# Start addresses of the weight buffers in SBUF: 0 modulo 512 bytes, or odd multiples of 16

## The chip, the core and the metric

The kernel runs on one core of a Trainium2 chip. The metric is device time in microseconds, from the start to the end of one launch. TensorE (PE) multiplies, VectorE (DVE), ScalarE (ACT) and GpSimd (POOL) do the work between the products, SyncE (SP) issues nearly all DMAs. SBUF is the on-chip memory that all engines read; PE writes its sums to PSUM.

## The reference

Attention with 4 sink tokens and a window of 128 over 4 x 8 heads, then a mixture of 8 experts over the 3072 tokens that it gives, every expert on every token, weighted by a Sinkhorn-normalised gate:

```python
x = attn_out.transpose(0, 2, 1, 3).reshape(3072, 512)
P = exp(x @ w_gate - max);  8 times: rows to sum 1, columns to sum N / E
for e in range(8):
    h = np.maximum(x @ w1[e], 0.0)        # 512 -> 1024
    out += P[:, e:e+1] * (h @ w2[e])      # 1024 -> 512
```

All of it is float32.

## The kernel before, in words

The tokens are worked in three parts of 1024; the code numbers them 0, 1, 2, and the change speaks of the second and third of these (`part` 1 and 2 in the code). Each expert's 1024 hidden columns are cut into four units of 256, so a part has 32 units. Both products of a unit are done by a Strassen-Winograd scheme with seven smaller products, M1 to M7. Each number is held as a float32 pair, high and low (`fp32r` tiles with an index of 2 in them), and a product is the sum of three terms: high by high, high by low, low by high.

In the first part the sums of weight blocks that the scheme needs (the weights' forms) are made on the chip and stored in DRAM (`w1s`, `w2s`). In the other two parts they are only loaded again, one form at a time, 128 partitions by 2 KB. The first product's form goes to a buffer of pool `w1q` (8 buffers, tile name W1q, issued in `load_w1`), the second product's form to a buffer of pool `w2q` (16 buffers, tile name W2q, issued in `load_w2`). A buffer that has been used is loaded again at once for a later product.

Each matmul has its own 128x128 block of weights: it is loaded into the array by an LDWEIGHTS (PEld in the profile) while the matmul before it runs, and then 512 columns of the other operand stream past it. In these parts the weights are always slices of W1q or W2q. What streams is a form of x for the first product (tiles B11, B21, B22, T1 to T4; line L902, in `product`), and a form of the hidden values for the second (tiles hf, pool `hq`; line L1467, in `second2`). One Strassen product is six such matmuls, and the blocks of one buffer lie 512 bytes apart:

```python
TERMS = [(0, k, b) for k in range(KH) for b in range(2)] + [(1, k, 0) for k in range(KH)]
    for j, (a, k, b) in enumerate(TERMS):
        nc.tensor.matmul(ps, lhsT=w1(a, k), rhs=x[:, b, k, :], ...)
```

The six of the second product take three from each of two units' buffers. The order of the work is written out by hand (`ORDER`, `SECOND`, `STEPS2`, and `at`, which puts an action some steps later), so nothing in it depends on addresses. Two unused tiles, `pad` and `base`, bring the pools on the left and on the right side of SBUF to multiples of 512 bytes: in the built program every tile that PE reads in the three parts (W1f, W2f, h, W1q, W2q, hf and the forms of x) starts at 0 modulo 512.

The attention ahead of the parts has tiles that don't. The scores (L498, in `scores`) take keys as the streaming operand and queries as the weights from one tile KQ, which holds for each of two (high, low) and two pairs of heads a row of 516 floats: 260 of keys, then 256 of queries. Two heads go side by side on 64 partitions each, so matmuls come in pairs. The transposes of the probabilities (L530, in `transpose_p`) take as weights `sc[:, h, SINK:]` for eight heads, whose rows are 132 floats (528 bytes) long; what streams there is always the same identity matrix.

Of the kernel before, what the change touches and what calls it, by code (L numbers as in the profile page):

```python
# [10 lines left out]
F32R = mybir.dt.float32r  # L11
# [5 lines left out]
P = 128  # L17
# [221 lines left out]
def tile_sink_attention_moe(ctx: ExitStack, tc: tile.TileContext, q, k, v, wg, w1, w2, out):  # L239
# [15 lines left out]
    KH = KC // 2  # L255
# [7 lines left out]
    def f32(ap):  # L263
        return ap.bitcast(F32)
# [118 lines left out]
    for hh in range(2):  # L383
        t = att2.tile([P, NP, CW + 2 * P], F32, name=f"KQF{hh}")
# [520 lines left out]
    HD = DM // 2  # L905
    weighted = []
    W1Q = {}
# [34 lines left out]
    w1p, cp, rawp, sp, xrp = (pool_(*a) for a in (("w1p", 1), ("cp", 1), ("rawp0", 2), ("sp", 2), ("xrp", 1)))  # L942
# [393 lines left out]
    with ExitStack() as p1:  # L1336
        pool_ = lambda name, bufs, **kw: p1.enter_context(tc.tile_pool(name=name, bufs=bufs, reuse_waits="tile", **kw))
        W1N, W2N = 8, 16
        w1p, pb, cp, wp, hp = pool_("w1q", W1N), pool_("pb", 2), pool_("cq", 1), pool_("wq", 6), pool_("hq", 16)
        ORDER = ["M2", "M1", "M5", "M3", "M6", "M7", "M4"]  # L1340
        units1 = [(e, u) for e in range(E) for u in range(NU)]
        NJ = len(units1)
# [3 lines left out]
        W2Q = {}  # L1346
        coming1 = iter([(part, n, m) for part, n in jobs1 for m in ORDER if (part, n, m) not in W1Q])
        first_ones = set(W1Q)

        def load_w1(k):  # L1350
            for _ in range(k):
                key = next(coming1, None)
                if key:
                    part, n, m = key
                    t = W1Q[key] = w1p.tile([P, 2, KH, P], F32R, name="W1q")
                    nc.sync.dma_start(f32(t).rearrange("p w k f -> p w (k f)"), w1s[units1[n]][:, FA[W1_OF[m]]])

        W2_OF = {"M1": "B11", "M2": "B21", "M3": "B22", "M4": "T4", "M5": "T1", "M6": "T2", "M7": "T3"}
# [11 lines left out]
        def load_w2(k):  # L1370
            for _ in range(k):
                key = next(coming2, None)
                if key:
                    part, n, m = key
                    t = W2Q[key] = w2p.tile([P, 2, HD], F32R, name="W2q")
                    nc.sync.dma_start(f32(t), w2s[units1[n]][:, FORMS.index(W2_OF[m])])

        PBS = {}
# [13 lines left out]
        def first2(part, n):  # L1392
# [4 lines left out]
            def run(m):  # L1397
                c = "c2" if m in ("M2", "M5", "M3") else "c1"
                start = m in ("M2", "M1", "M5")
                if start:  # L1400
                    T[c] = ps0.tile([P, HT], F32, name=c)
                W = W1Q.pop((part, n, m))
                product(T[c], lambda a, k: W[:, a, k, :], XF[READS[m]], start, True)
                if (part, n, m) not in first_ones:
                    at(1, lambda: load_w1(1))
                if (part, n) == (1, NJ - 1):
                    at(1, lambda: load_form(m))
# [48 lines left out]
        def second2(part, group):  # L1456

            begin, end = group[0] == 0, group[-1] == NJ - 1
            for m, k in order_of(group):
# [11 lines left out]
                def then(m=m, k=k, o=o, hold=hold):  # L1471
                    if hold:
                        sums[m, k] = o
                    elif end and (m, k) == ("M3", 1):
                        for cols in HALVES if part == 2 else (slice(0, HT),):
                            nc.vector.tensor_add(sums["M6", k][:, cols], o[:, cols], sums["M6", k][:, cols])
                    elif begin:
                        t = sums[m, k] = (accq if (m, k) in FEW else accp).tile([P, DM], F32, name="acc")
                        nc.scalar.copy(t, o)
                    else:  # L1480
                        nc.vector.tensor_add(sums[m, k], o, sums[m, k])  # L1481
                    if end:
                        together(part, m, k)
                        if (m, k) == ("M4", 1):
                            at(2 if part == 2 else 3, lambda: put_out(part, 1))
                        if part == 1 and (m, k) == ("M3", 1):
                            at(2, lambda: put_out(part, 0))
                        if part == 2 and m in ("M2", "M3"):

                            d = 2 * (m == "M3") + k  # L1490
                            at(1 if d == KC - 1 else 2, lambda d=d: last_out(d, ("c1", "c2", "held1", "held3")[d]))
                    if (m, k) != ("M3", 1) and k == 1 or (m, k) == ("M3", 0) and not end or (m, k) == ("M3", 1) and end:
                        at(1, lambda: load_w2(len(group)))
# [92 lines left out]
        def second_pools():  # L1586
            nonlocal w2p, accq
            p0r.close()
            w2p, accq = pool_("w2q", W2N, side="right"), pool_("accq", 3, side="right")
            load_w2(W2N)  # L1590

        w2p = accq = None
        load_weights(1, 0)
        load_w1(W1N)
        unit(1, 0, last_second, BEGIN[0])
        unit(1, 1, last_second, BEGIN[1][:-1] + [second_pools] + BEGIN[1][-1:])
# [46 lines left out]
```

## Time and profile before

| | |
|---|---|
| median of two executions | 2079.61 us (2079.07 and 2080.16) |
| span of the profiled execution, first to last instruction | 2077.3 us |
| PE busy | 2060.9 us, 99% of the span |
| DVE, ACT, POOL busy | 70%, 40%, 34% |
| granted TensorE clock, mean | 0.999 |

The time of the profiled execution itself is not listed apart; its span is 1.8 to 2.9 us below the two executions' times. A matmul's busy time in the profile includes a tail that overlaps the next matmul, so its mean duration (389 ns) is not the rate: the rate is read from where matmuls start.

### The profile page before, as it was taken

Reading aid. Unit: us, or ns where it says so; the run is one execution under the profiler, and the core shown is the slowest. Engines: PE = TensorE matmul, PEld = TensorE weight load, DVE = VectorE, ACT = ScalarE, POOL = GpSimd, SP = SyncE. Lnnn points to the kernel's source line nnn. Section 1 sums busy time; section 2 is a strip of 40 time slices with the busy share of each in tenths; the row PEclk is TensorE's granted clock in tenths of the full one; section 3 lists DMA queues with packets and bytes.
Section 4 is the critical chain, followed back from the end, with each engine's and each line's share of the span. In section 5 each row is a group of like instructions: output and inputs, shape, how many; then the busy total and the mean of one; then the engine's idle time right before and its main releaser. Section 6 shows DMA issues by size and latency. Waiting matters only on the chain.

```text
span 2077.3 us, 31257 instructions
## 1 busy us (share of the span) xinstructions
PE 2060.9 (99%) x10407; PEld 1706.0 (82%) x10407; DVE 1462.4 (70%) x2732; ACT 840.2 (40%) x1787; POOL 713.7 (34%) x833
## 2 busy tenths in 40 slices
PE   8999999999999999999999999999999999999998
PEld 7888778888888888888888888888888888888887
DVE  6777688787877767756666666666666667666666
ACT  7877445444444444333323322332432232333222
POOL 7766523333333321322322232233332223222323
PEclk9999999999999999999999999999999999999999
DMA  7655269898989886766666666668766666666662
GB/s 178 161 118 120 85 211 323 288 319 291 315 282 323 289 274 223 280 211 197 199 203 198 204 205 191 202 207 334 224 208 194 200 205 191 207 203 202 197 193 83
DMA packets 397622, 453.78 MB, mean 218 GB/s; under 512 B 99664, under 2 KB 265744, under 8 KB 396560
## 3 DMA queue, kind: packets, MB, share of 16 engines
q1 hardware_dynamic: 397064, 451.57, 69.6%
q8 instruction: 85, 1.39, 0.3%
q14 instruction: 81, 0.66, 0.1%
q10 hardware_dynamic: 392, 0.16, 0.0%
HBM read 314.17 MB, written 137.46 MB: 217 GB/s over the span
## 4 chain that ended last, share of the span: by engine, by line
PE 96%; DVE 2%; ACT 1%; POOL 0%; issue 0%; DMA 0%; SPq 0%; DVEq 0%; ACTq 0%; POOLq 0%
PE c L902 42%; PE o L1467 21%; PE held L1467 8%; PE held L1152 7%; PE o L1152 7%; PE st L638 2%; PE st L652 2%; PE st L572 2%; PE st L498 2%; PE st L457 1%; PE st L530 1%; PE st L580 0%; DVE sc L508 0%; DVE st L507 0%; PE st L603 0%
## 5 line engine op out<-in xcount | busy, mean ns | idle before, releaser
L928 ACT CAST hf<-w 128x512 fp32r<-128x512 f32 x448 | 265.3, 621 | 562.2 <-POOL w L1434 299.7
L1467 PE MATMUL o<-hf,W2q 128*128 128x512 f32 x1920 | 472.0, 389 | 0.0
L1467 PEld LDWEIGHTS o<-hf,W2q 128*128 128x128 f32 x1920 | 360.0, 188 | 75.5 <-DVE acc L1481 0.9
L902 PE MATMUL c<-T,W1q 128*128 128x512 f32 x1530 | 388.8, 389 | 0.2 <-DVE w L1415 0.2
L931 DVE TENSOR_TENSOR hf<-w,hf 128x512 fp32r<-128x512 f32 x448 | 329.1, 763 | 75.6 <-ACT hf L928 68.0
L902 PEld LDWEIGHTS c<-T,W1q 128*128 128x128 f32 x1530 | 286.8, 188 | 60.7 <-DVE w L1415 0.9
L1481 DVE TENSOR_TENSOR acc<-o,acc 128x512 f32<-128x512 f32 x298 | 204.6, 687 | 169.9 <-PE o L1467 169.9
L902 PE MATMUL c<-B,W1q 128*128 128x512 f32 x1134 | 278.3, 389 | 0.0
L1434 POOL TENSOR_TENSOR w<-w 128x512 f32<-128x512 f32 x64 | 82.7, 1293 | 492.0 <-DVE w L1416 492.0
L902 PEld LDWEIGHTS c<-B,W1q 128*128 128x128 f32 x1134 | 212.5, 188 | 44.0
L1415 DVE TENSOR_TENSOR w<-c,M 128x512 f32<-128x512 f32 x192 | 132.2, 689 | 139.9 <-PE c L902 135.6
L1411 ACT COPY M<-c 128x512 f32<-128x512 f32 x192 | 112.8, 587 | 249.1 <-PE c L902 249.0
L1467 PE MATMUL held<-hf,W2q 128*128 128x512 f32 x768 | 194.8, 389 | 0.0
L1152 PE MATMUL held<-W2f,h 128*128 128x512 f32 x672 | 171.1, 390 | 0.0
L902 PE MATMUL c<-T,W1f 128*128 128x512 f32 x672 | 171.0, 390 | 0.1
L1152 PE MATMUL o<-W2f,h 128*128 128x512 f32 x672 | 170.5, 389 | 0.1
L1467 PEld LDWEIGHTS held<-hf,W2q 128*128 128x128 f32 x768 | 144.0, 188 | 29.8
L1449 POOL TENSOR_TENSOR w<-w 128x512 f32<-128x512 f32 x64 | 106.3, 1661 | 176.0 <-DVE hf L931 176.0
L1152 PEld LDWEIGHTS o<-W2f,h 128*128 128x128 f32 x672 | 126.0, 188 | 27.0 <-DVE acc L1159 0.9
L902 PEld LDWEIGHTS c<-T,W1f 128*128 128x128 f32 x672 | 125.8, 188 | 26.9 <-issue 0.5
L1152 PEld LDWEIGHTS held<-W2f,h 128*128 128x128 f32 x672 | 125.8, 188 | 26.4 <-DVE W2f L931 0.5
L961 POOL TENSOR_TENSOR r<-r 128x256 f32<-128x256 f32 x27 | 20.1, 745 | 367.8 <-ACT M L1115 231.4
(216 smaller groups left out, 2740.3 us busy)
## 6 DMA issues: line engine op xcount, KB each, us to landing
W2q<-w2s SPq DMA_DIRECT2D x448, 256.0 KB, 3.1
W1q<-w1s SPq DMA_DIRECT2D x444, 256.0 KB, 2.8
w1s<-W1f SPq DMA_DIRECT2D x56, 896.0 KB, 7.7
w2s<-WT SPq DMA_DIRECT2D x136, 256.0 KB, 3.2
r<-in_moe_w_dram SPq DMA_DIRECT2D x64, 512.0 KB, 5.5
w2s<-W2f SPq DMA_DIRECT2D x56, 256.0 KB, 5.7
PB<-psd SPq DMA_DIRECT2D x16, 512.0 KB, 4.0
w2s<-W2f SPq DMA_DIRECT2D x56, 128.0 KB, 7.8
```

What stands on the lines that cost most here:

```text
L498: nc.tensor.matmul(ps[hh * HH + 2 * pr + r][:, 0:w], lhsT=Q[rows, a, pr, :], rhs=K[rows, c, pr, 0:w], start=(j == 0), stop=(j == len(terms ...
L572: nc.tensor.matmul(O[r * D:(r + 1) * D, c], lhsT=x_[:, 2 * c + r], rhs=y_[:, 2 * c + r], start=(j == 0 and c == 0), stop=(j == len(ops) - ...
L902: nc.tensor.matmul(ps, lhsT=w1(a, k), rhs=x[:, b, k, :], start=(start and j == 0), stop=(stop and j == len(TERMS) - 1), skip_group_check=n ...
L928: nc.scalar.copy(dst[:, 0], src)
L931: low_ = nc.vector.tensor_sub(dst[:, 1], src, f32(dst[:, 0])).ins
L1152: nc.tensor.matmul(o, lhsT=h[c, th][:, a, off:off + P], rhs=W2F[n][:, w, c, :], start=(begin and c == 0 and j == 0), stop=(end and c == 1 ...
L1411: nc.scalar.copy(t, T["c2"])
L1415: nc.vector.tensor_add(w, T["c1"], T[m])
L1434: nc.gpsimd.tensor_sub(S3, T["A11"], T["A21"])
L1449: at(k, lambda: nc.gpsimd.tensor_sub(T["A11"], w, T["A11"]))
L1467: nc.tensor.matmul(o, lhsT=W2Q[part, n, m][:, a, k * P:(k + 1) * P], rhs=F[part, n, H_OF[m]][:, w, :], start=(j == 0 and (begin or not hol ...
L1481: nc.vector.tensor_add(sums[m, k], o, sums[m, k])
```

## The change

The two pools' buffers get a gap, and the data starts 4 floats (16 bytes) into each. The gap is 16 floats for W1q and 8 for W2q, so that the buffers are 2112 and 2080 bytes apart instead of 2048.

```diff
+        def spaced(pool, gap, name):
+            return pool.tile([P, 2 * HD + gap], F32R, name=name)[:, 4:4 + 2 * HD]
...
-                    t = W1Q[key] = w1p.tile([P, 2, KH, P], F32R, name="W1q")
+                    t = W1Q[key] = spaced(w1p, 16, "W1q").rearrange("p (w k f) -> p w k f", w=2, k=KH)
...
-                    t = W2Q[key] = w2p.tile([P, 2, HD], F32R, name="W2q")
+                    t = W2Q[key] = spaced(w2p, 8, "W2q").rearrange("p (w d) -> p w d", w=2)
```

In the built program the data of the 8 W1q buffers starts at 16, 80, 144, ... 464 modulo 512, that of the 16 W2q buffers at 16, 48, 80, ... 496. Both pools grow by 512 bytes in all, so that the pools behind them move by 512 and still start at 0 modulo 512; what streams past the weights stays at 0 modulo 512 throughout. The first four forms of part 1 (tile WT, 24 matmuls) are not in these pools and stay where they were.

The instructions of every engine stand in the same order as before. What differs is a few waits on SP, where a buffer now lies over another tile of the part before: the first load of PB waits for PE as well, and among the first 16 loads of W2q these waits stand one place earlier. On SP, at the change to part 1, before (a name in brackets is what the DMA waits for: an earlier DMA, or an engine that used the place):

```order
L1376 DMA W2q<-w2s_4751 128x512 [waits DMAHW2_49]
L1376 DMA W2q<-w2s_5704 128x512 [waits DMAHW3_49]
L1376 DMA W2q<-w2s_4751 128x512 [waits DMAHW4_49]
L1376 DMA W2q<-w2s_5704 128x512 [waits DMAHW5_49,PE_49]
L1376 DMA W2q<-w2s_4751 128x512 [waits DMAHW6_49]
L1376 DMA W2q<-w2s_5704 128x512 [waits DMAHW7_49]
L1376 DMA W2q<-w2s_4751 128x512 [waits DMAHW0_49]
L1376 DMA W2q<-w2s_5704 128x512 [waits DMAHW1_49,PE_49,Activation_49]
```

The same eight loads in the changed kernel:

```order
L1381 DMA W2q<-w2s_4751 128x512 [waits DMAHW2_49,Activation_49]
L1381 DMA W2q<-w2s_5704 128x512 [waits DMAHW3_49]
L1381 DMA W2q<-w2s_4751 128x512 [waits DMAHW4_49,PE_49]
L1381 DMA W2q<-w2s_5704 128x512 [waits DMAHW5_49]
L1381 DMA W2q<-w2s_4751 128x512 [waits DMAHW6_49]
L1381 DMA W2q<-w2s_5704 128x512 [waits DMAHW7_49]
L1381 DMA W2q<-w2s_4751 128x512 [waits DMAHW0_49,PE_49]
L1381 DMA W2q<-w2s_5704 128x512 [waits DMAHW1_49]
```

PE's two waits have moved from the fourth and eighth load to the third and seventh, and ACT's from the eighth to the first.

## Rows read from the trace of the kernel before

**Rows 1.** The page: busy time, and the chain that ended last.

```profile
PE 2060.9 (99%) x10407; PEld 1706.0 (82%) x10407; DVE 1462.4 (70%) x2732; ACT 840.2 (40%) x1787; POOL 713.7 (34%) x833
...
PE 96%; DVE 2%; ACT 1%; POOL 0%; issue 0%; DMA 0%; SPq 0%; DVEq 0%; ACTq 0%; POOLq 0%
```

**Rows 2.** Groups by line: matmuls with weights from W1q or W2q.

```profile
L1467 PE MATMUL o<-hf,W2q 128*128 128x512 f32 x1920 | 472.0, 389 | 0.0
...
L902 PE MATMUL c<-T,W1q 128*128 128x512 f32 x1530 | 388.8, 389 | 0.2 <-DVE w L1415 0.2
...
L902 PE MATMUL c<-B,W1q 128*128 128x512 f32 x1134 | 278.3, 389 | 0.0
...
L1467 PE MATMUL held<-hf,W2q 128*128 128x512 f32 x768 | 194.8, 389 | 0.0
```

**Rows 3.** The chain, 860 to 900 us: start, time until the next piece, what.

```profile
866.19 1.36 PE held L1467 x6
867.55 1.36 PE c L902 x6
868.91 1.36 PE o L1467 x6
```

**Rows 4.** Windows: stretch, its length, engines' busy time (instructions), clock, DMA share.

```profile
839.80:2068.90 1229.10, 1228.87 (x5443) 1016.02 (x5442) 829.52 (x1215) 386.65 (x671) 372.81 (x268) 1.00 0.65 206
```

```profile
870.00:1430.00 560.00, 560.00 (x2473) 463.68 (x2472) 374.75 (x551) 174.20 (x302) 163.06 (x118) 1.00 0.67 211
```

**Rows 5.** Timeline, PE, one span's scores without its first pair; then the last pair.

```profile
130.37 1.47 PE L498 MATMUL st<-KQ 64*128 64x260 f32 x22
```

```profile
131.56 0.28 PE L498 MATMUL st<-KQ 64*128 64x260 f32 x2
```

**Rows 6.** Timeline, PE, from 248.4 us: nine matmuls soon after a pause.

```profile
248.23 2.24 PE L638 MATMUL st<-B,W 128*128 128x512 f32 x9
```

**Rows 7.** Timeline, PE, 200.6 to 201.3 us: transposes of eight heads' probabilities.

```profile
200.43 1.04 PE L530 MATMUL st<-ident,sc 128*128 128x128 f32 x8
```

**Rows 8.** Loads: KB each, median us to landing.

```profile
W2q<-w2s SPq DMA_DIRECT2D x448, 256.0 KB, 3.1
W1q<-w1s SPq DMA_DIRECT2D x444, 256.0 KB, 2.8
```

**Rows 9.** Timeline of SP and of PE where W2q is first loaded and used.

```profile
862.24 8.78 SPq L1376 DMA_DIRECT2D W2q<-w2s  x16
```

```profile
866.03 1.52 PE L1467 MATMUL held<-hf,W2q 128*128 128x512 f32 x6
```

## Prediction

> **What bounds the kernel.** I read the page first: PE is busy for 99% of the span, and the chain that ended last is PE for 96% [rows 1]. In the stretch that the change touches, the window over it shows PE busy for 1228.87 of 1229.1 us at a granted clock of 1.00, which is the upper of its two levels, 2.4 GHz [rows 4]. So no engine and no transfer holds PE up there; only the rate at which PE takes its own matmuls can. That rate is not the 389 ns in the groups by line [rows 2], which has an overlapping tail in it. The chain has it: every six matmuls take 1.36 us, 226.7 ns each [rows 3]. The second window confirms it: 2473 matmuls are seen in 560 us, two or so of them cut by its edges, so 560 / 2471 = 226.6 ns [rows 4].
>
> Now the floor: 512 columns at 2.4 GHz take 213.3 ns. Each matmul thus pays 13.3 ns that is not streaming, although PE waits for nobody and the next weights are being loaded beside it. The matmuls with weights from W1q or W2q are 1920 + 1530 + 1134 + 768 = 5352 [rows 2]. They pay 5352 x 13.3 = 71 us in all, 3.4% of the time. That is all that this change can win, and the question is whether those 13.3 ns depend on where the weights start.
>
> **What the trace says of addresses.** Three places bear on it.
>
> First, the scores. Their weights (queries) and streaming columns (keys) lie in one tile, with rows of 516 floats: the queries start 1040 bytes behind the keys, 16 modulo 512, and the next row is 16 bytes further again. The weights loaded during a matmul are the next pair's, and in the ten steps of a span that I look at they lie 16 bytes off the running keys (modulo 512) seven times and 32 or 64 three times. So this is the one place with weights mostly at odd multiples of 16 from what streams. The ten pairs from 130.37 to 131.56 us [rows 5] take 1.19 / 10 = 119 ns each, of which 260 columns at 2.4 GHz are 108.3. They pay 10.7 ns, against 13.3 where all lies at 0. That is 2.6 ns less (1.6 to 3.6 with the rounding of two starts to 10 ns). The comparison is not clean: each matmul there uses 64 partitions, and two run side by side.
>
> Second, matmuls with everything at 0 modulo 512 that come soon after a pause. The nine from 248.23 us [rows 6] take (2.24 - 0.39) / 8 = 231 ns each, 4.6 ns more than in the steady stretch, with tiles aligned just as well. So the 13.3 ns is not a fixed price of a weight change. It is the price of a rhythm into which the steady stream falls after some eight matmuls, and PE pays about 18 ns until then. Streaming and weight loading evidently get in each other's way, by how they are timed against each other.
>
> Third, the transposes. Their weights move by 528 bytes from head to head, so every second one starts at an odd multiple of 16, while the same identity streams. The eight start (1.04 - 0.27) / 7 = 110 ns apart without a sign of it [rows 7]. There only 128 columns stream for each load, of another format, so this speaks for indifference but only weakly.
>
> On the page "SBUF — State Buffer" of the Trainium skill, section "Who interferes with whom", PE is given two independent read ports, one for the moving operand and one for LDWEIGHTS, and is said never to wait on anyone. By that rule the start address would change nothing; the two rates of identical matmuls in rows 4 and 6 don't fit a PE whose two reads never meet, while rows 7 do.
>
> **The change, part by part.**
> - Weights at odd multiples of 16. The nearest row is the scores: 2.6 ns less for each matmul. 5352 x 2.6 = 14 us less (9 to 19 us with the rounding). The bounds are the floor of 213.3 ns, 71 us less, and the rate after a pause, 5352 x 4.3 to 4.6 = 23 to 25 us more. I take the scores' value, because it is the only row with such offsets.
> - Each buffer at another offset. Within one product of six the offset is the same for all blocks of a buffer, since they lie 512 bytes apart. If only the place modulo 32 matters, all 24 buffers are alike and the change from one to the next costs nothing. If more of the address matters, the rhythm is disturbed every three or six matmuls; that is the slower rival below.
> - Loads. They are the same 892 loads of 2 KB for each partition, now to places that are not multiples of 32. DMA engines are busy for 0.65 of the stretch [rows 4], and a load lands 2.8 to 3.1 us after its issue [rows 8], while a W1q buffer is needed again only after eight products of 1.36 us and the second products among them. What hides a slower write is this lead and the free 0.35. I count 0; without the cover it is the last rival.
> - Waits on SP. PE's wait stands one load earlier, and ACT's at the first. The 16 loads are issued in 8.78 us, 0.55 each, from 862.24, and the first matmul on W2q starts at 866.03 [rows 9]. The six matmuls there need the first two loads; the third is needed a product later. A load held for one place is 0.55 us later, inside that lead. 0, and at most about 1 us, once. PB's extra wait is for old reads of the first part, which is also 0.
> - Pools moved by 512 bytes keep their place modulo 512: 0.
>
> The sum against the profiled execution is 2077.3 - 14 = 2063.3 us of span. The listed executions lie 1.8 to 2.9 us above the span, 2.3 at the median, which gives 2065.6; I say **2065 us**.
>
> **The rivals.**
> - *Nothing happens.* The 13.3 ns then come from the timing of the two reads alone, or all 24 buffers shift the rhythm alike. Rows 7 speak for it, and so does that products on quite different tiles keep the same 1.36 us [rows 3]; the 10.7 ns of the scores speak against it. It gives 2077 to 2083 us.
> - *The rhythm is lost.* The steady 226.7 ns is reached only after some eight equal matmuls in a row [rows 6]. In the changed kernel the offset changes after every product, and within the second product between two buffers. If the offset decides the rhythm beyond 32 bytes, it never settles, and 231 ns is paid throughout. That is 5352 x 4.5 = 24 us more, 2104 us; it is slower than before as soon as the mean rate exceeds 226.7, and by 2% from 234.5 ns on, which the mean of rows 6 doesn't reach. For it: the scores, whose offsets also change from pair to pair, have no settled rhythm to show for their 119 ns. Against it: they pay less, not more.
> - *Nearly all of it goes.* If weights one line off never meet the stream, the matmul comes near its 213.3 ns. At 219 ns the gain is 41 us (2038 us), at the floor 71 us (2008 us). No matmul of the rows comes so near; even the scores pay 10.7. "TensorE: Matmul & The Clock Gate" of the Trainium skill, section "Wait — 56ns, not 53.3ns?", gives 215.7 ns for warm back-to-back matmuls of 512 columns; by this figure the estimate would be 5352 x 11 = 59 us less, 2021 us. No row of this case shows that rate.
> - *The loads become the bound.* If a write that doesn't start at a multiple of 32 took more than 1 / 0.65 = 1.54 times as long, the DMA engines could not keep up. At twice the time for the loads, which are 234 of the stretch's 206 x 1.229 = 253 MB, the share would be 0.65 x 1.92 = 1.25 and the stretch 0.25 x 1229 = 307 us longer. Nothing in the trace shows such a write.
>
> **Chances and range.** The forecast (2055 to 2071, down to 2044 if the gain is nearer 6 ns) gets 0.38, nothing 0.23, the lost rhythm 0.23, nearly all gone 0.13, loads 0.03. The predicted time is that of the first. Its neighbours on both sides belong in the range: from 2036, which leaves out nearly all of the fourth, to 2106, which takes in the third at its price. Left out are some 0.18. Faster by over 2% (under 2038; 2% is about what a measurement of this kernel can tell from no change) comes from the fourth case and a sliver of the first: 0.15. Slower by over 2% (over 2121) is the loads and the worst of the lost rhythm, 0.07. The rest is 0.78. As to sign alone, the cases below the old time have 0.51, those above it 0.26.
>
> **What would show it.** In the chain of the changed kernel, six matmuls should take 1.34 to 1.35 us, and the window from 870 to 1430 us should hold about 2500 matmuls instead of 2473. Pieces of 1.36 us again mean that nothing happened. About 1.39 us, and 2425 in the window, mean the lost rhythm, and 1.28 to 1.31 that most of the price is gone. The first part, whose weights are not moved, must keep 1.36 in every case; if it does not, something else than the offset has changed. Slower loads would show as a longer time to landing and, if they bind, as idle time of PE that a DMA ends. I would be wrong above all if the scores' lower price comes from their 64 partitions or their pairing and not from the offset.

## The result and the profile after

| | before | after |
|---|---|---|
| median of two executions | 2079.61 us | 2108.23 us (2108.17 and 2108.29) |
| span of the profiled execution | 2077.3 us | 2106.6 us |
| ratio after to before | | 1.0139, 95% interval 1.011 to 1.0168 |

The change makes the kernel slower by 28.6 us. The page of the changed kernel, its busy times and the engines of the chain that ended last:

```profile
PE 2088.5 (99%) x10407; PEld 1707.8 (81%) x10407; DVE 1465.9 (70%) x2732; ACT 840.2 (40%) x1787; POOL 715.4 (34%) x833
...
PE 95%; DVE 2%; ACT 1%; POOL 0%; issue 0%; DMA 0%; SPq 0%; DVEq 0%; ACTq 0%; POOLq 0%
```

PE does the same 10407 matmuls as in [rows 1] and is still busy for 99% of the span. Its idle time goes from 16.4 us (2077.3 - 2060.9) to 18.1, so nearly all of the loss is PE's work itself, which got longer. The chain from 860 to 900 us, against [rows 3]:

```profile
866.37 1.41 PE held L1472 x6
867.78 1.40 PE c L902 x6
869.17 1.39 PE o L1472 x6
870.56 1.41 PE c L902 x6
```

Six matmuls take 1.39 to 1.41 us where they took 1.36 (further on in this chain two sixes keep 1.36). The windows give the mean, for the stretch of [rows 4] and for one in the first part, whose weights were not moved; the last line is the same stretch of the first part before (PE busy and its instructions, PEld, DVE, ACT, POOL, clock, DMA share, GB/s):

```profile
870.00:1430.00 560.00, 560.00 (x2416) 453.83 (x2415) 368.01 (x538) 171.62 (x297) 160.68 (x116) 1.00 0.66 201
310.60:632.00 321.40, 321.40 (x1419) 266.14 (x1418) 247.09 (x383) 149.03 (x277) 99.83 (x121) 1.00 0.92 305
310.60:632.00 321.40, 321.40 (x1420) 266.13 (x1419) 247.49 (x382) 148.99 (x277) 99.42 (x121) 1.00 0.92 305
```

Two matmuls are cut by a window's edges, so this is 560 / 2414 = 232.0 ns against 226.6 before, at the same granted clock of 1.00. In the first part it is still 321.4 / 1417 = 226.8 ns. The difference of 5.4 ns on 5352 matmuls is 28.9 us, about the whole loss. The first and last start of a group of these matmuls, before and after, say the same:

```profile
L1467 PE MATMUL o<-hf,W2q x1920: 388/389/501, 868.8 to 2068.6; 128*128 128x512 f32 x192
L1472 PE MATMUL o<-hf,W2q x1920: 387/394/476, 869.0 to 2095.9; 128*128 128x512 f32 x192
```

The first matmul on W1q starts at 839.9 us before and at 839.8 after. So the stretch with the moved weights takes 1256.1 us instead of 1228.7, 27.4 us more, out of 29.3 by which the two spans differ. The other 2 us pass after the last matmul (8.9 us against 6.9; 6.6 to 7.4 in the twelve other profiles of this case), and nothing here ties them to the change. The loads show nothing, against [rows 8] and [rows 9]:

```profile
W2q<-w2s SPq DMA_DIRECT2D x448, 256.0 KB, 3.1
W1q<-w1s SPq DMA_DIRECT2D x444, 256.0 KB, 2.9
```

```profile
862.44 8.70 SPq L1381 DMA_DIRECT2D W2q<-w2s  x16
```

They land after 3.1 and 2.9 us (before 3.1 and 2.8), the DMA share is 0.66 (0.67), and the 16 first loads of W2q go out in 8.70 us (8.78), whatever their waits.

### The profile page after: what moved, and what is told of

It is laid out like the page before. It is cut to its first block, busy times and chain, and to the rows that moved or that the text cites. A ratio compares the mean times of both kernels' runs of the same rounds, so it can differ in the third digit from the quotient of the medians.

```text
span 2106.6 us, 31256 instructions
## 1 busy us (share of the span) xinstructions
PE 2088.5 (99%) x10407; PEld 1707.8 (81%) x10407; DVE 1465.9 (70%) x2732; ACT 840.2 (40%) x1787; POOL 715.4 (34%) x833
## 3 DMA queue, kind: packets, MB, share of 16 engines
q8 instruction: 86, 1.41, 0.3%
## 4 chain that ended last, share of the span: by engine, by line
PE 95%; DVE 2%; ACT 1%; POOL 0%; issue 0%; DMA 0%; SPq 0%; DVEq 0%; ACTq 0%; POOLq 0%
PE c L902 42%; PE o L1472 21%; PE held L1472 8%; PE held L1152 7%; PE o L1152 7%; PE st L652 2%; PE st L638 2%; PE st L572 2%; PE st L498 2%; PE st L457 1%; PE st L530 1%; DVE sc L508 0%; PE st L580 0%; DVE st L507 0%; PE st L603 0%
## 5 line engine op out<-in xcount | busy, mean ns | idle before, releaser
L1472 PE MATMUL o<-hf,W2q 128*128 128x512 f32 x1920 | 481.7, 394 | 0.0
L902 PE MATMUL c<-T,W1q 128*128 128x512 f32 x1530 | 396.9, 395 | 0.2 <-DVE w L1420 0.2
L902 PE MATMUL c<-B,W1q 128*128 128x512 f32 x1134 | 284.4, 395 | 0.0
```

Source lines behind the costliest of these rows:

```text
L902: nc.tensor.matmul(ps, lhsT=w1(a, k), rhs=x[:, b, k, :], start=(start and j == 0), stop=(stop and j == len(TERMS) - 1), skip_group_check=n ...
L1472: nc.tensor.matmul(o, lhsT=W2Q[part, n, m][:, a, k * P:(k + 1) * P], rhs=F[part, n, H_OF[m]][:, w, :], start=(j == 0 and (begin or not hol ...
```

## The experiments

Three theories stood at the beginning. "Changing": the rhythm is lost because the offset changes from buffer to buffer. "Odd": weights at an odd multiple of 16 bytes from the stream cost more as such. "Far": only offsets far from 0 modulo 256 lose the rhythm. The runs came in three groups, and each is set against the kernel before as timed with its group: medians of 2079.2, 2079.0 and 2079.3 us. "Rate" below is the mean time from one matmul's start to the next one's.

**few16: one offset for all, 16 bytes.** In the changed kernel:

```diff
-        W1N, W2N = 8, 16
+        W1N, W2N = 6, 12
-                    t = W1Q[key] = spaced(w1p, 16, "W1q")...
+                    t = W1Q[key] = spaced(w1p, 128, "W1q")...
-                    t = W2Q[key] = spaced(w2p, 8, "W2q")...
+                    t = W2Q[key] = spaced(w2p, 128, "W2q")...
```

> All weight buffers of parts 1 and 2 start at the same 16 bytes modulo 512 (6 and 12 buffers of 2560 bytes instead of 8 and 16, since more do not fit). Theory 'changing': the rhythm is lost because the offset changes from buffer to buffer; here it does not, so 226.7 ns per matmul, 2077 to 2084 us. Theory 'odd': weights at an odd multiple of 16 from the stream cost about 232 ns as such; 2104 to 2110 us. Theory 'far': only offsets far from 0 modulo 256 lose the rhythm; 16 is near, so 2077 to 2084 us. Fewer buffers may cost a few us by themselves, which few0 shows.

**few0: the same buffers at 0.** The diff of few16 and `[:, 0:2 * HD]` in `spaced`.

> The same 6 and 12 buffers of 2560 bytes, all at 0 modulo 512. All three theories: 226.7 ns per matmul, 2077 to 2084 us; what is above the kernel before is the price of fewer buffers.

few0 took 2079.13 us, ratio 1.000 (0.999 to 1.0009): fewer buffers cost nothing. few16 took 2105.1 us, ratio 1.011 (1.0069 to 1.0152), and its four executions fell into two kinds, 2096.91 and 2096.97, 2113.23 and 2113.63. The profiled one took 2113.23:

```profile
920.00:1400.00 480.00, 480.00 (x2059) 388.72 (x2058) 318.94 (x467) 143.22 (x247) 135.06 (x97) 1.00 0.64 196
```

480 / 2057 = 233.3 ns, and in the trace's start times the same six gaps (233, 235, 233, 234, 233, 232 ns) come again and again for 480 us. Of the other kind only the time is known: (2096.9 - 2079.1) / 5352 = 3.3 ns more than few0 for each matmul, a mean rate of 230.0. A rhythm of 230.0 throughout would give it, but so would 233.3 in one of the two parts and 226.7 in the other (2676 x 6.7 = 17.8 us), and no trace tells which. So one constant offset is enough to lose the 226.7, and there is a rhythm, only a slower one, or even two. "Changing" is not needed to explain the loss.

**even: spaced, at even multiples of 16.** In the changed kernel `[:, 0:2 * HD]` in `spaced`.

> The buffers spaced as in the changed kernel, but the data at the start of each: 0, 64, ... 448 for W1q and 0, 32, ... 480 for W2q, all even multiples of 16. Theory 'odd': 226.7 ns, 2077 to 2084 us. Theory 'changing': about 232 ns, 2103 to 2110 us. Theory 'far': most offsets are as far as in the changed kernel, so 2100 to 2110 us.

2105.89 us, ratio 1.0127 (1.011 to 1.0144). "Odd" falls: without any odd multiple the price is nearly the same, 26.7 us.

**const128: one even offset, far away.** In the kernel before, pads put all W1q and W2q at 128:

```diff
+        pool_("g1", 1).tile([P, 32], F32, name="g1")
+        w1p = pool_("w1q", W1N)
+        pool_("g2", 1).tile([P, 96], F32, name="g2")
...
+            pool_("g3", 1, side="right").tile([P, 96], F32, name="g3")
+            w2p = pool_("w2q", W2N, side="right")
+            pool_("g4", 1, side="right").tile([P, 32], F32, name="g4")
```

> 8 and 16 buffers of 2048 bytes, all at 128 modulo 512. Theory 'changing' and theory 'odd': 226.7 ns per matmul, 2077 to 2084 us. Theory 'far': the weights are as far from the stream as they get modulo 256, so no rhythm at 226.7; 230 to 234 ns, 2095 to 2118 us.

2110.98 us, ratio 1.0151 (1.0134 to 1.0168), the slowest of all by its median, with no change of offset anywhere and the buffers' number and pitch as before. Part 1 and part 2 settle differently:

```profile
920.00:1400.00 480.00, 480.00 (x2067) 389.15 (x2067) 318.86 (x469) 143.11 (x247) 135.20 (x97) 1.00 0.64 196
1560.00:2000.00 440.00, 440.00 (x1887) 353.95 (x1886) 293.49 (x429) 130.22 (x224) 126.41 (x91) 1.00 0.63 194
```

480 / 2065 = 232.4 ns and 440 / 1885 = 233.4 ns. "Far" alone predicted this one, but it had missed few16. I formed a new theory, "own rate": each offset of the weights against the stream settles at a rate of its own.

**sweep_even and sweep_odd: 32 offsets, one after the other.** In the diff of few16, each four units in a row get an offset:

```diff
+        def spaced(pool, part, n, name):
+            k = ((part - 1) * NJ + n) // 4
+            off = 8 * k            # sweep_odd: 8 * k + 4
+            return pool.tile([P, 2 * HD + 128], F32R, name=name)[:, off:off + 2 * HD]
```

> 6 and 12 buffers of 2560 bytes; all weights of four units in a row (some 76 us) start at the same offset, and the offset goes up by 32 bytes from each four units to the next, 0 to 480 over the 16 stretches. Theory 'only 0': the first stretch runs at 226.7 ns per matmul, each other one at 230 to 234; about 2100 to 2112 us in all. Theory 'by distance': 226.7 also at 256, and a slow rise and fall between. A rival that would make a better kernel: some offset settles below 226.7, at 220 or less.

> The same with 16 bytes more in each stretch, 16 to 496. Theory 'only 0': 230 to 234 ns in all 16 stretches, 2100 to 2115 us. Theory 'by distance': 226.7 to 228 at 16, 240, 272 and 496, more between. The rival: some odd multiple of 16 settles below 226.7 ns.

They took 2106.97 and 2106.02 us (one execution each). The rates, from the start times in the traces where the weights of the twelve matmuls around have the same offset (second half of each such stretch, 70 to 110 matmuls):

```
offset modulo 256     0    16    32    48    64    80    96   112   128   144   160   176   192   208   224   240
first time        226.7 233.3 233.3 233.3 233.3 232.0 234.3 233.3 232.3 233.3 233.3 230.0 228.9 231.9 233.3 226.7
256 bytes later   226.7 233.3 233.3 233.3 233.3 232.0 234.3 233.3 232.3 233.3 233.3 230.0 228.9 231.9 233.3 227.0
```

(The last stretch, 496, has the pauses at the kernel's end in it.) The chain of sweep_even shows two of these stretches, 128 and 192 bytes:

```profile
1187.97 1.40 PE held L1474 x6
1189.37 1.39 PE o L1474 x6
1190.75 1.39 PE c L902 x6
```

```profile
1344.02 1.37 PE held L1474 x6
1345.39 1.37 PE o L1474 x6
1346.77 1.37 PE c L902 x6
```

The two rows of the table agree, so the offset counts modulo 256 bytes. It is neither parity nor a smooth distance: 240, an odd multiple of 16, is as good as 0 in this run, and 16, its neighbour on the other side, is among the worst. No multiple of 16 is better than 0.

**all128: weights and stream moved together.** In the kernel before the unused tiles get other sizes:

```diff
-    const.tile([P, 8], F32, name="pad")
+    const.tile([P, 40], F32, name="pad")
-    base.tile([P, 120], F32, name="base")
+    base.tile([P, 88], F32, name="base")
```

> The kernel before with all its tiles moved by 128 bytes modulo 512 (pad and base sized anew), weights and stream alike. Theory 'relation': only the offset of weights against stream counts, so 226.7 ns and 2077 to 2084 us. Theory 'place': the weights or the stream must themselves start at 0 modulo 512; 230 to 234 ns in all three parts, 2105 to 2140 us.

2079.41 us, ratio 1.0001 (0.9991 to 1.0011). The window of [rows 4] holds as many matmuls as before:

```profile
870.00:1430.00 560.00, 560.00 (x2472) 463.69 (x2471) 374.70 (x551) 174.44 (x302) 163.01 (x118) 1.00 0.67 211
```

With the same weights at 128 that cost 31.8 us in const128, nothing is lost when the stream lies at 128 too. What counts is the relation of the two. The loads go to the same places modulo 512 in both runs, so it is not they. But nearly every other tile has moved with the stream, and that the relation is to the stream, and not to what another engine reads or writes, is argued only: the gaps of few16 repeat for 480 us while the other engines' work changes beside them.

**w2only and w1only: half of the change each.** In the changed kernel the line of `load_w1`, or of `load_w2`, is the one of before.

> Only the W2q buffers are spaced, W1q lies at 0 as before. If each matmul pays for its own weights: 2688 x 5.3 ns = 14 us more, 2090 to 2096 us, with W1q's matmuls at 226.7. If the rhythm belongs to the stream of matmuls as a whole and is upset every six of them: nearly the whole price, 2100 to 2108 us, with W1q's matmuls above 229 ns as well.

> Only the W1q buffers are spaced (16, 80, ... 464), W2q lies at 0. Own rates of these eight offsets by the sweep: 233.3, 232.0, 233.3, 231.9 twice, mean 232.6, so 2664 x 5.9 = 16 us more if W2q's matmuls keep 226.7 ns; as with W2q alone, some 5 us more come from W2q's matmuls that need time to settle: 2094 to 2102 us.

w2only took 2095.71 us, ratio 1.008 (1.0063 to 1.0097), w1only 2095.0 us, ratio 1.0076 (1.0059 to 1.0093). The windows from 870 to 1430 us, w2only and then w1only:

```profile
870.00:1430.00 560.00, 560.00 (x2438) 457.64 (x2437) 370.38 (x544) 174.00 (x302) 161.17 (x116) 1.00 0.66 205
```

```profile
870.00:1430.00 560.00, 560.00 (x2439) 457.64 (x2439) 369.61 (x543) 174.15 (x302) 161.09 (x116) 1.00 0.66 205
```

Both run at 560 / 2436 = 229.9 ns. The halves cost 16.8 and 15.7 us, together 32.5 against the whole change's 28.6. The expectation for w2only, 2090 to 2096 us with W1q's matmuls at 226.7, held in its time and not in its detail: by the start times, the matmuls after which weights at 0 follow took 228.9 ns, and in w1only 228.6. A matmul at 0 that follows others does not settle at once. w1only stayed in its expected range too, near the lower end: of the 16 + 5 us in its expectation 15.7 came. There the matmuls that load weights at 16 took 227.1 ns, where the sweep has 233.3: among others an offset need not keep the rate that it settles at by itself.

**few240: one offset for all, 240 bytes, an odd multiple of 16.** The diff of few16 with `[:, 60:60 + 2 * HD]`.

> As few16, but all weight buffers at 240 modulo 512, an odd multiple of 16. Theory 'own rate' (each offset of weights against stream settles at a rate of its own, the same 256 bytes further, 226.7 ns at 0 and at 240): 2077 to 2084 us, with 226.7 ns throughout. A rival by which any odd multiple of 16 costs: 2100 us or more.

2088.0 us, ratio 1.0043 (1.0026 to 1.006): three executions at 2087.95 to 2088.23, and the profiled one at 2083.68. The profiled one, in the windows of part 1 and part 2:

```profile
920.00:1400.00 480.00, 480.00 (x2104) 394.38 (x2103) 324.01 (x478) 145.28 (x250) 139.14 (x100) 1.00 0.65 199
1560.00:2000.00 440.00, 440.00 (x1943) 364.34 (x1942) 298.55 (x439) 134.28 (x232) 128.16 (x93) 1.00 0.65 199
```

480 / 2102 = 228.4 ns in part 1 and 440 / 1941 = 226.7 ns in part 2. So at 240 there are two rhythms within one execution. (2088.0 - 2079.1) / 5352 = 1.7 ns is what the slower one in both parts would give; that the slower executions stayed in it is likely, but their traces were not kept. "Own rate" holds only if an offset may have more than one, as 128 has in const128. The expected range missed the median by 4 us; the rival's 2100 us or more was further off.

**good4: an offset that changes all the time, among four good ones.** In the diff of few16:

```diff
+        count = {}
+        def spaced(pool, name):
+            j = count[name] = count.get(name, -1) + 1
+            off = (0, 60, 64, 124)[j % 4]
+            return pool.tile([P, 2 * HD + 128], F32R, name=name)[:, off:off + 2 * HD]
```

> 6 and 12 buffers of 2560 bytes, whose offsets go 0, 240, 256, 496 from one load to the next, so that it changes with nearly every product and, in the second product, every three matmuls; but each of the four settles at 226.7 ns by itself. Theory 'own rate': 2077 to 2086 us. Theory 'changing' (a change of offset alone upsets the rhythm): 2095 to 2110 us.

2079.5 us, ratio 1.0001 (0.9992 to 1.0011), and the window of [rows 4] again:

```profile
870.00:1430.00 560.00, 560.00 (x2471) 463.57 (x2471) 374.18 (x550) 174.99 (x303) 162.82 (x117) 1.00 0.67 209
```

560 / 2469 = 226.8 ns. Half of these weights lie at odd multiples of 16 and the offset changes with every buffer, and it costs nothing. "Changing" falls by this run, and "odd" a second time.

**sweep_fine: offsets within a line of 16 bytes.** The sweep's diff with a list of 16 offsets.

> As the two sweeps, with offsets 4, 8, 12, 20, 24, 28, 40, 56, 200, 216, 228, 232, 236, 244, 248, 252, which are no multiples of 16. If reads go by lines of 16 bytes, an offset within a line costs one more line for each load, 228 to 236 ns; near 0 and 256 the best of them stays at 226.7. The rival, which would make a better kernel: one of them settles below 226.7 ns.

2105.56 us (one execution). The rates, found as above (252 by its matmuls ahead of the pauses at the end):

```
offset    4     8    12    20    24    28    40    56   200   216   228   232   236   244   248   252
rate  232.4 230.6 233.3 233.3 231.1 235.0 233.3 233.3 230.7 232.1 226.7 231.1 231.7 233.3 233.3 226.7
```

No offset settles below 226.7 ns. Two that are no multiples of 16, 228 and 252, reach it as well, so an offset within a line of 16 bytes need not cost anything. Of these 48 offsets (32 of them different modulo 256) none makes a better kernel than the one before.

## Why the prediction was wrong

- **What bounds the kernel** was read rightly. PE's own rate is all there is to win or lose, 27.4 of the 29.3 us between the two spans lie in the stretch of the 5352 matmuls counted, and the first part kept its rate.
- **The step that failed** is the price taken for "weights at odd multiples of 16": 2.6 ns less for each matmul, from the scores [rows 5]. Measured was 5.1 to 5.3 ns more (27.4 or 28.6 us over 5352). The scores' weights lie 16, 32 or 64 bytes off what streams; with whole 512-column matmuls the sweeps give 233.3 ns for all three (few16's faster executions have 230.0 on the mean). So the sign was wrong, and not only the size. The scores use 64 partitions, two matmuls side by side and 260 columns; I named the first two as a weakness and took the value all the same, because it was the only row with such offsets. Which of them makes the scores cheap was not tried. Fewer columns alone hardly do it: the kernel before has matmuls of 256 columns on all 128 partitions (line L638, all at 0 modulo 512), and fifteen of them in a row take 1.96 us from 43.06 us on at a granted clock of 1.00, so they start (1.96 - 0.28) / 14 = 120 ns apart. 256 columns at 2.4 GHz are 106.7 ns, and the 13.3 above them are the same as for 512 columns.
- **The upper bound** was too low. I took 231 ns, the mean of the matmuls after a pause [rows 6], as the price of a lost rhythm. Settled rates up to 235.0 exist. The range ended at 2106 us and the time is 2108.23.
- **The rival "the rhythm is lost"** had nearly the right size (2104 us; the signs named for it were 1.39 us and 2425 matmuls in the window, and 1.39 to 1.41 and 2416 came) and half of the mechanism: 226.7 is a rhythm that weights and stream fall into, and it was lost. Its condition was wrong. It is not the change of offset after every product (good4 changes it as often and loses nothing; const128 never changes it and loses 31.8 us). What decides is which offsets occur and, in a mixture, beside which others.
- **"If only the place modulo 32 matters"** is answered: it counts modulo 256, and within 32 bytes too. The mean loss comes out near what the sweeps add up to. W1q's eight offsets (16, 80, 144 and 208 modulo 256) average 232.6 ns, W2q's sixteen (the odd multiples of 16) 231.7: 2664 x 5.9 + 2688 x 5.0 = 29 us, against 27.4 to 28.6 measured. The same sum for even gives 24 us against 26.7. It is a sum of settled rates, and that it fits so well is in part luck, for in the mixture single offsets differ from their own rates both ways: in the changed kernel matmuls that load weights at 240 took 229.5 ns, not 226.7, and those at 16 took 231.3, not 233.3.
- **Loads, waits on SP and moved pools** were rightly counted at nothing: the loads land in the same time to 0.1 us, and few0, with fewer buffers and gaps between them, keeps the old time.
- **The two read ports.** The page "SBUF — State Buffer" of the Trainium skill, section "Who interferes with whom", calls PE's two read ports independent and says that PE never waits on anyone. The measurement doesn't agree with what I took from it, that start addresses change nothing: const128 differs from the kernel before in where tiles start, with the same work on PE, and is 31.8 us slower. That PE waits for another engine no run here shows. The transposes [rows 7], which seemed to say the same as the rule, did not carry over to these matmuls.

What stays open is why an offset has its rate: that the two reads of PE meet is inferred from all128 against const128, but whether they do, and at which place in the memory or in the engine, was not shown. Nor is it known what decides which of two rhythms the matmuls fall into at 128 or 240 bytes, or whether 16 is a third such case.

## What to carry to other kernels

Where PE is the bound and streams 512 columns of this format for each load of weights, put weights and stream at the same place modulo 256 bytes, and keep padding that does so when a tile is added: here the start addresses alone are worth 1.5%. Don't price such an edit by a row of another shape or pairing, even if it is the only one with the right offsets. Several offsets can be measured in one run, one to each stretch of a long uniform kernel, and that tells more than several kernels with one guess each. But a stretch shows one rhythm only: 240 gave 226.7 ns in the sweep and 228.4 in a part of few240.

## What the runs showed of the hardware

The rate at a constant offset is not noisy but a cycle that repeats exactly, of one to seven matmuls at most offsets (a few have longer ones): 226.7 alone; 232, 226, 229 at 192 bytes; 229, 226, 229, 236 at 176 (start times to the nanosecond). The cycles' sums are whole multiples of 6.67 ns: 34 of them for 226.67, 103 for three matmuls at 228.89, 138 for four at 230.0, 174 for five at 232.0, 105 for three at 233.33, 246 for seven at 234.29. So the price of an offset comes in steps, and a shift of 4 bytes (228 to 232) can cost 4.4 ns for each matmul. The same offset at the same granted clock of 1.00 can settle in two such cycles: 228.4 and 226.7 ns in the two parts of one execution of few240, 232.4 and 233.4 in those of const128. That the executions of few16 lie 16.5 us apart (2096.9 and 2113.2 to 2113.6) looks like an unsteady measurement and is likely the same thing, but only the slower kind has a trace.
